# One-query attention over 16 heads on one core: single-head loops with register addresses in place of unrolled pairs

## The chip, the core and the metric

The kernel runs on one NeuronCore of a Trainium2 chip. A core has five engines, each with a queue of its own: TensorE (PE; the profile shows weight loads apart, as PEld), VectorE (DVE), ScalarE (ACT), GpSimd (POOL) and SyncE (SP). In front of each engine a sequencer reads the instructions. It carries out register arithmetic, branches and waits itself and hands the rest to the engine. Rows of the sequencers have a q behind the engine's name (DVEq, ACTq, SPq; PEldq for PE). Data moves between the device memory and the core's SBUF by DMA, sixteen transfer engines that all queues share. [...]

The metric is the device time of one execution, in microseconds; lower is better.

## The reference

One query row per head attends to 8192 keys and values of 256 elements, for 16 heads, in bfloat16:

```python
B, H, Sq, Sk, D = 1, 16, 1, 8192, 256

def reference(q, k, v):
    scale = q.shape[-1] ** -0.5
    scores = jnp.einsum("bhqd,bhkd->bhqk", q, k) * scale
    p = _softmax(scores, axis=-1)
    return jnp.einsum("bhqk,bhkd->bhqd", p, v)
```

K and V are 67 MB each and every element is used once, so the kernel is a stream: 8.39 MB of K and V per head.

## The kernel before

A head's 8192 keys lie as 128 partitions by J = 64 columns of 256 elements; a partition reads 64 consecutive keys. K and V each have two buffers of a whole head (`kbuf0/1`, `vbuf0/1`), taken in turn.

*Transfers.* SP issues all of K and V in a fixed list (`stream`): after a prologue always K of head h+2, then V of head h. A load waits until its buffer is free: K for `kd`, counted when DVE has done the last column of head h-2 of that buffer, V for `pv`, counted by the last P.V matmul (L136). The last heads' V comes in pieces (`V_LATE`), down to two columns at the end.

*Scores.* DVE takes columns 0 to 47 of a head: one instruction per column multiplies the key with the query and sums over the 256 elements (L191, followed by a read of the accumulator), written in place and into `S`. PE takes the other 16, in four groups of four: transpose (L280), copy of the transposes to SBUF by ACT (L376), product with the query as a column (L294), copy of the 16 scores to `S` (L380).

*Softmax.* DVE takes the maximum over `S` (L207), PE transposes it (L228), DVE reduces it to one number (L173), PE spreads it to all partitions (L234), ACT negates it and takes the exponential with a running sum (L384, L388). PE adds the sum over partitions (L244), DVE inverts it (L178).

*Values.* 64 matmuls of one weight column each accumulate P.V (L259) into `acc`; ACT scales the result (L401) and issues a store of 512 B for each head (L408).

*Order.* Every engine has a hardware loop over pairs of heads. A turn is written out for an even and an odd head, so buffers, columns and semaphores of each are constants in the instructions; only wait values, and a few addresses on ACT, are computed in registers. PE's turn is: scores of the even head, P.V of the previous pair's even head, scores of the odd head, P.V of the previous pair's odd head. `_Step` works out the wait values, `AHEAD` counts semaphores up before the loops so that the first turns do not stall. The queue that an instruction stands in is its engine's; nothing is reordered but by the lines below.

## Time and profile before

| | |
|---|---|
| median of 3 runs | 320.04 us (320.0 to 320.32) |
| span of the profiled execution | 318.6 us |
| instructions in it | 6833 |
| PE, PEld, DVE, ACT, POOL busy | 219.2, 156.0, 275.2, 92.5, 1.6 us |
| moved by DMA | 134.29 MB, mean 422 GB/s |
| issue to landing of a whole K, of a whole V | 20.3 us, 28.7 us |
| scores by DVE (L191) | 268.4 us busy |
| P.V (L259) | 147.1 us busy |
| copies of the transposes (L376) | 62.3 us busy |

The profile is one execution; the metric is the median of runs without it, and the execution's own time is the span and what lies around it. In a group's row stand the line, the engine, the operation, the tile that is written and those that are read, the shapes, the count, then busy time and mean duration, then the idle time before the group and what ended it. A row of one line's instructions gives the smallest, median and largest duration in ns and the first and last start in us. A timeline row gives start, duration and count. The waits say who waited for whom: us in total, times, the longest. A window's row gives the stretch, the busy time of PE, PEld, DVE, ACT and POOL with counts, the granted share of TensorE's clock, DMA's share and GB/s. Register and branch instructions have rows but are not counted as busy.

### The profile page before, as it was taken

How to read it: one execution, taken by the hardware profiler on the slowest of the kernel's cores; microseconds unless marked ns; L12 is line 12 of the kernel's file. 1: busy time of each engine (PE TensorE's matmuls, PEld its weight loads, DVE VectorE, ACT ScalarE, POOL GpSimd, SP SyncE). 2: the span in 40 equal slices, each digit the busy share in tenths (PEclk: the TensorE clock that was granted, in tenths of full speed). 3: DMA queues.
4: the chain of work that ended last, by engine and by line, in shares of the span. 5: the costliest groups of instructions: out<-in, count | busy, mean ns of one | idle time of the engine just before them, and what ended most of it. 6: DMA issues, size and time to landing. Idle time of an engine off the chain costs nothing.

```text
span 318.6 us, 6833 instructions
## 1 busy us (share of the span) xinstructions
PE 219.2 (69%) x2163; PEld 156.0 (49%) x2163; DVE 275.2 (86%) x1584; ACT 92.5 (29%) x172; POOL 1.6 (0%) x11
## 2 busy tenths in 40 slices
PE   4446185988775947949387482975739668497987
PEld 1335163656553634727256262663626446266664
DVE  3989999999999898897988979799798897979920
ACT  5436050333215050330505114051330603306010
POOL 1000000000000000000000000000000000000000
PEclk9999999659797875957879597695977859699999
DMA  7999999999999999999999999999999999999995
GB/s 303 447 418 465 393 455 407 448 416 448 412 448 428 428 444 411 453 412 453 420 436 440 416 448 407 453 416 449 424 432 444 411 449 416 444 405 428 419 416 201
DMA packets 6981, 134.29 MB, mean 422 GB/s; under 512 B 800, under 2 KB 1216, under 8 KB 1856
## 3 DMA queue, kind: packets, MB, share of 16 engines
q1 hardware_dynamic: 6912, 134.22, 98.6%
q8 instruction: 2, 0.03, 0.0%
q10 hardware_dynamic: 64, 0.02, 0.0%
q14 instruction: 3, 0.02, 0.0%
HBM read 134.23 MB, written 0.01 MB: 421 GB/s over the span
## 4 chain that ended last, share of the span: by engine, by line
DMA 64%; PE 19%; DVE 15%; SPq 1%; issue 1%; ACT 0%; DVEq 0%; ACTq 0%
DMA vbuf<-in_v_dram 58%; PE acc L259 18%; DVE kbuf L191 14%; DMA kbuf<-in_k_dram 7%; SPq L136 1%; DVE S L191 0%; DVE g L173 0%; PE sm L234 0%; ACT o_sb L401 0%; DVE recip L178 0%; DVEq L209 0%; DVEq L183 0%; PE qps L244 0%; DVE m L207 0%; ACTq L400 0%
## 5 line engine op out<-in xcount | busy, mean ns | idle before, releaser
L191 DVE CUSTOM_DVE_ANT_0 kbuf<-kbuf,q_now 128x256 bf16<-128x256 bf16 x768 | 268.4, 409 | 21.3 <-DMA kbuf<-in_k_dram 20.4
L259 PE MATMUL acc<-vbuf,E 128*1 128x256 bf16 x1024 | 147.1, 313 | 41.6 <-DMA vbuf<-in_v_dram 41.4
L259 PEld LDWEIGHTS acc<-vbuf,E 128*1 128x1 bf16 x1024 | 95.5, 95 | 86.2 <-DMA vbuf<-in_v_dram 44.4
L376 ACT ACTIVATE KT<-tp 128x1024 bf16<-128x1024 bf16 x64 | 62.3, 1021 | 46.4 <-PE tp L280 45.9
L191 DVE DVE_READ_ACCUMULATOR2_ANT S<- 128x1 f32 x768 | 55.2, 72 | 0.0
L280 PE MATMUL tp<-identb,kbuf 128*128 128x128 bf16 x512 | 42.2, 239 | 14.7 <-DMA kbuf<-in_k_dram 14.5
L280 PEld LDWEIGHTS tp<-identb,kbuf 128*128 128x128 bf16 x512 | 33.6, 107 | 18.1 <-DMA kbuf<-in_k_dram 12.1
L294 PE MATMUL spe<-q_now,KT 128*128 128x1 bf16 x512 | 22.9, 166 | 27.3 <-ACT KT L376 27.0
L294 PEld LDWEIGHTS spe<-q_now,KT 128*128 128x128 bf16 x512 | 18.1, 99 | 35.7 <-ACT KT L376 26.1
L401 ACT ACTIVATE o_sb<-acc,recip 1x256 bf16<-1x256 f32 x16 | 7.3, 458 | 87.0 <-PE acc L259 85.7
L384 ACT ACTIVATE negb<-sm 128x1 f32<-128x1 f32 x16 | 2.8, 174 | 83.8 <-PE sm L234 83.8
L173 DVE TENSOR_REDUCE g<-mx 1x1 f32<-1x128 f32 x16 | 4.4, 276 | 7.5 <-PE mx L228 7.5
L234 PE MATMUL sm<-g,ones_row 1*128 1x1 f32 x32 | 6.5, 268 | 5.0 <-DVE g L173 5.0
L228 PE MATMUL mx<-ident,m 128*1 128x128 f32 x32 | 6.5, 287 | 4.3 <-DVE m L207 4.3
L234 PEld LDWEIGHTS sm<-g,ones_row 1*128 1x128 f32 x32 | 5.1, 198 | 7.1 <-DVE g L173 5.6
L371 ACT ACTIVATE q_now<-q_all 128x258 bf16 x16 | 6.7, 418 | 0.1
L178 DVE RECIPROCAL recip<-qps 1x1 f32<-1x1 f32 x16 | 2.4, 152 | 3.9 <-PE qps L244 3.9
L388 ACT ACTIVATE E<-S,negb 128x64 bf16<-128x64 f32 x16 | 5.6, 348 | 0.5
L336 PE MATMUL acc<-q_sb,identb 16*128 16x256 bf16 x16 | 4.3, 404 | 0.8 <-ACT q_all L426 0.8
L228 PEld LDWEIGHTS mx<-ident,m 128*1 128x1 f32 x32 | 2.1, 82 | 5.1 <-DVE m L207 4.8
L426 ACT ACTIVATE q_all<-acc 128x512 bf16<-128x512 f32 x8 | 4.3, 592 | 0.6 <-PE acc L336 0.6
L380 ACT ACTIVATE S<-spe 128x16 f32<-128x16 f32 x16 | 2.9, 184 | 3.6 <-PE spe L294 3.6
(24 smaller groups left out, 18.5 us busy)
## 6 DMA issues: line engine op xcount, KB each, us to landing
kbuf<-in_k_dram SPq DMA_DIRECT2D x15, 4096.0 KB, 20.3
vbuf<-in_v_dram SPq DMA_DIRECT2D x11, 4096.0 KB, 28.7
vbuf<-in_v_dram SPq DMA_DIRECT2D x6, 2048.0 KB, 24.4
vbuf<-in_v_dram SPq DMA_DIRECT2D x5, 1024.0 KB, 14.8
kbuf<-in_k_dram SPq DMA_DIRECT2D x2, 1024.0 KB, 5.8
kbuf<-in_k_dram SPq DMA_DIRECT2D x1, 2048.0 KB, 11.3
vbuf<-in_v_dram SPq DMA_DIRECT2D x1, 768.0 KB, 10.2
vbuf<-in_v_dram SPq DMA_DIRECT2D x1, 640.0 KB, 11.3
```

Of the source, the lines that this page charges most:

```text
L173: dve.tensor_reduce(g[0:1, h.par : h.par + 1], mx[0:1, 0:P], AX.X, ALU.max).then_inc(sem("g"), 1)
L191: ins = dve.tensor_tensor_reduce(out=buf[:, j * D : (j + 1) * D], in0=buf[:, j * D : (j + 1) * D], in1=q_now[h.par][:, 0:D], scale=SCALE, ...
L228: pe.matmul(mx[0:1, 0:P], lhsT=m[:, h.par : h.par + 1], rhs=ident[:, :], start=True, stop=True).then_inc(sem("mT"), 1)
L234: pe.matmul(sm[:, 0:1], lhsT=ones_row[0:1, 0:P], rhs=g[0:1, h.par : h.par + 1], start=True, stop=True,).then_inc(sem("bc"), 1)
L259: ins = pe.matmul(acc[h.par][0:1, 0:D], lhsT=E[h.par][:, j : j + 1], rhs=vbuf[h.par][:, j * D : (j + 1) * D], start=(j == 0), stop=(j == J ...
L280: ins = pe.transpose(tp[gi % 2][:, b * D + hf * P : b * D + (hf + 1) * P], buf[:, j * D + hf * P : j * D + (hf + 1) * P], identb[:, :],)
L294: ins = pe.matmul(spe[:, c : c + 1], lhsT=KT[gi % 2][:, b * D + hf * P : b * D + (hf + 1) * P], rhs=q_now[h.par][:, D + hf : D + hf + 1], ...
L336: ins = pe.matmul(acc[pair % 2][:, (h % 2) * D : (h % 2 + 1) * D], lhsT=identb[0:H, h : h + 1].to_broadcast([H, P]), rhs=q_sb[:, :], start ...
L371: act.activation(out=q_now[h.par][:, :], in_=src_q, func=ACT.Copy).then_inc(sem("qb"), 1)
L376: act.activation(out=KT[gi % 2][:, :], in_=tp[gi % 2][:, :], func=ACT.Copy).then_inc(sem("kt"), 1)
L388: act.activation(out=E[h.par][:, :], in_=S[h.par][:, :], func=ACT.Exp, bias=negb[:, h.par : h.par + 1], scale=1.0, accum_out=lsum[:, h.par ...
L401: act.activation(out=o_sb[h.par][0:1, :], in_=acc[h.par][0:1, 0:D], func=ACT.Copy, scale=recip[0:1, h.par : h.par + 1],).then_inc(sem("fin ...
```

## The change: one head per turn, addresses computed

All four loops now run over single heads. Buffers become one tile of two halves (`kbuf`, `vbuf`, `acc`), `S` and `E` keep all heads, and the place within them is computed in registers from the loop's counter. The parts:

- DVE has an inner loop of six times eight columns; the instruction is `scalar_tensor_tensor` in place of `tensor_tensor_reduce`; the query comes from `q_all` and not from a copy per head. Maximum and reciprocal of earlier heads stand after the second eight. K is freed by the maximum (`m`) and no longer by the last column.
- PE has H + 2 turns: scores of head h, P.V of head h-2 as an inner loop of sixteens, the sum of head h-1. A product with zeros opens each accumulation.
- GpSimd waits for each load in the order of the list and counts it in one of two counters, `kc` (units of eight columns) and `vc` (units of two), for which DVE and PE wait.
- ACT has no query copies per head, and keeps the 16 results in `o_sb`, which one DMA stores at the end.

```diff
-K_FIRST = (16, 32)
-V_LATE = {14: (0, 16, 32, 48), 15: (0, 16, 28, 38, 46, 52, 57, 60, 62)}
+CH = 8
+PC = 16
+V_STEPS = (0, 4, 8, 12, 14)
...
+    15: (0, 16, 28, 40, 46, 52, 56, 60, 62),
+AHEAD = {"vc": 64, "sc": 1, "sp": 2, "m": 1, "pv": 2, "fin": 4, "rc": 3, "l": 2, "qs": 2}
...
-                            sp.wait_ge(sem("kd"), h)
+                        sp.wait_ge(sem("m"), h)
...
+            def landed(kind, name, value, columns):
+                pool.wait_ge(sem(name), value)
+                if kind == "k":
+                    pool.nop().then_inc(sem("kc"), columns // CH)
+                else:
+                    pool.nop().then_inc(sem("vc"), columns // 2)
...
+            with dve.Fori(0, H) as h:
+                par = dve.snap(h % 2)
+                qh = q_all[:, ds(h * D, D)]
+                with dve.Fori(0, NC) as c:
+                    dve.wait_ge(sem("qs"), h // 2 + 3)
+                    dve.wait_ge(sem("kc"), h * KC + c + 1)
+                    for b in range(CH):
+                        col = kbuf[:, ds(par * (J * D) + c * (CH * D) + b * D, D)]
+                        ins = dve.scalar_tensor_tensor(
+                            out=col,
+                            in0=col,
+                            scalar=SCALE,
+                            in1=qh,
                             op0=ALU.mult,
-                            op1=ALU.add,
-                            accum_out=S[h.par][:, j : j + 1],
+                            op1=ALU.mult,
+                            accum_out=S[:, ds(h * J + c * CH + b, 1)],
                         )
                     ins.then_inc(sem("kd"), 1)
+                    with dve.If(c == 1):
+                        with dve.If(h > 0):
+                            xmax(Head(h, 1))
+                        with dve.If(h > 1):
+                            recips(Head(h, 2))
+                dve.wait_ge(sem("kd"), h * NC + NC)
+                dve.wait_ge(sem("sc"), h + 2)
+                dve.tensor_reduce(m[:, :], S[:, ds(h * J, J)], AX.X, ALU.max).then_inc(sem("m"), 1)
...
+            def ktrans(at, gi):
+                for b in range(GRP):
+                    for hf in range(NH):
+                        ins = pe.transpose(
+                            tp[gi % 2][:, b * D + hf * P : b * D + (hf + 1) * P],
+                            kbuf[:, ds(at + (JD + gi * GRP + b) * D + hf * P, P)],
+                            identb[:, :],
+                        )
+                ins.then_inc(sem("tp"), 1)
...
+            with pe.Fori(0, H + 2) as h:
+                with pe.If(h < H):
+                    now = Head(h)
+                    at = pe.snap((h % 2) * (J * D))
+                    with pe.If(h > 0):
+                        transpose_m(Head(h, 1))
+                    pe.wait_ge(sem("kc"), h * KC + KC)
+                    ktrans(at, 0)
+                    ktrans(at, 1)
+                    kscore(now, 0)
+                    with pe.If(h > 0):
+                        bcast(Head(h, 1))
+                    for gi in range(2, NG):
+                        ktrans(at, gi)
+                        kscore(now, gi - 1)
+                    kscore(now, NG - 1)
+                with pe.If(h > 1):
+                    o = pe.snap(Head(h, 2).i)
+                    par = pe.snap(o % 2)
+                    to = acc[0:1, ds(par * 512, D)]
+                    pe.wait_ge(sem("fin"), h + 1)
+                    pe.matmul(to, lhsT=zero[:, 0:1], rhs=zero[:, :], start=True, stop=False)
+
+                    def columns(c, stop):
+                        for b in range(PC):
+                            if b in V_STEPS:
+                                units = (V_STEPS + (PC,))[V_STEPS.index(b) + 1] // 2
+                                pe.wait_ge(sem("vc"), h * VU + c * (PC // 2) + units)
+                            ins = pe.matmul(
+                                to,
+                                lhsT=E[:, ds(o * J + c * PC + b, 1)],
+                                rhs=vbuf[:, ds(par * (J * D) + c * (PC * D) + b * D, D)],
+                                start=False,
+                                stop=stop and b == PC - 1,
+                            )
+                        return ins
+
+                    with pe.Fori(0, J // PC - 1) as c:
+                        columns(c, False)
+                        with pe.If(h == H):
+                            with pe.If(c == 1):
+                                transpose_m(Head(H - 1))
+                            with pe.If(c == 2):
+                                bcast(Head(H - 1))
+                    ins = columns(J // PC - 1, True)
+                    ins.then_inc(sem("pv"), 1)
+                with pe.If(h > 0):
+                    with pe.If(h < H + 1):
+                        total(Head(h, 1))
...
-                    act.dma_start(dst, o_sb[h.par][0:1, :]).then_inc(sem(f"o{h.par}"), 16)
+            act.wait_ge(sem("fin"), H + 4)
+            act.dma_start(out.rearrange("b h s d -> (b s) (h d)"), o_sb[:, :]).then_inc(sem("out"), 16)
+            act.wait_ge(sem("out"), 16)
```

How this stands in the instruction streams is shown at two places. On PE, the start of an odd head's P.V before (L259): two ISA rows, which compute values to wait for, and then matmuls in a row.

```order
L361 COMPARE_AND_BRANCH
L254 ISA
L255 ISA
L259 MATMUL acc<-vbuf,E 1x256 x16
L258 ISA
L259 MATMUL acc<-vbuf,E 1x256 x16
```

The same place of the changed kernel, from the inner loop's start (its lines 331 to 341 are `columns` and the loop around it in the diff).

```order
L341 UNCONDITIONAL_BRANCH
L341 ISA
L332 ISA x2
L332 MATMUL acc<-vbuf,E 1x256
L332 ISA
L332 MATMUL acc<-vbuf,E 1x256
L332 ISA
L332 MATMUL acc<-vbuf,E 1x256
L332 ISA
L332 MATMUL acc<-vbuf,E 1x256
L331 REGISTER_ALU
L332 ISA
```

Every matmul has an ISA row ahead of it. It folds the register operations that give the addresses of its column of `E` and of `vbuf` (add, multiply, add for each); a row of REGISTER_ALU ahead of some gives a value to wait for.

On DVE, within a head before: the branch around an earlier head's reciprocal, and a column (L191), which is the multiply with the sum and the read of the accumulator; the columns behind it follow with nothing between.

```order
L214 COMPARE_AND_BRANCH
L178 RECIPROCAL recip<-qps 1x1
L214 UNCONDITIONAL_BRANCH
L191 ISA kbuf,S<-kbuf,q_now 128x256
L191 ISA S 128x1
```

The start of the inner loop of the changed kernel (its line 214 is the column's instruction, 209 and 211 the loop and the wait).

```order
L209 ISA
L211 ISA
L214 ISA x3
L214 SCALAR_TENSOR_TENSOR kbuf,S<-kbuf,q_all 128x256
L214 ISA
L214 SCALAR_TENSOR_TENSOR kbuf,S<-kbuf,q_all 128x256
L214 ISA
L214 SCALAR_TENSOR_TENSOR kbuf,S<-kbuf,q_all 128x256
```

Here too an ISA row of six register operations stands ahead of each column, five rows stand at the start of each eight, and the loop's counter and two branches at its end.

## The prediction

> **What bounds the kernel now.** I read the page first (span, busy shares, the DMA row), then the chain of waits, then the middle of the run alone, then who waits for whom.

> ```profile
> span 318.6 us, 6833 instructions
> PE 219.2 (69%) x2163; PEld 156.0 (49%) x2163; DVE 275.2 (86%) x1584; ACT 92.5 (29%) x172; POOL 1.6 (0%) x11
> DMA  7999999999999999999999999999999999999995
> q1 hardware_dynamic: 6912, 134.22, 98.6%
> DMA 64%; PE 19%; DVE 15%; SPq 1%; issue 1%; ACT 0%; DVEq 0%; ACTq 0%
> 40.00:280.00 240.00, 169.04 (x1678) 120.48 (x1676) 219.55 (x1265) 68.86 (x126) 0.00 (x0) 0.79 1.00 432
> SPq L136 <- DVE S L191: 240.6, 14, 19.1
> PE acc L259 <- DMA vbuf<-in_v_dram: 41.4, 13, 4.7
> DVE kbuf L191 <- DMA kbuf<-in_k_dram: 20.4, 13, 5.5
> ```

> The transfer engines are full in every slice but the first and last. In the middle they move 432 GB/s; one head is 8.39 MB of K and V, so a head takes 8.39/432 = **19.4 us**, and sixteen of them make the run. SP sits in its waits for buffers only because it issues far ahead of a full queue. PE and DVE both wait for data. So the change is worth nothing until an engine needs more than 19.4 us per head; what each needs today:

> ```profile
> L191 DVE CUSTOM_DVE_ANT_0 kbuf<-kbuf,q_now 128x256 bf16<-128x256 bf16 x768 | 268.4, 409 | 21.3 <-DMA kbuf<-in_k_dram 20.4
> L259 PE MATMUL acc<-vbuf,E 128*1 128x256 bf16 x1024 | 147.1, 313 | 41.6 <-DMA vbuf<-in_v_dram 41.4
> 170.05 1.07 PE L280 MATMUL tp<-identb,kbuf 128*128 128x128 bf16 x16
> 175.03 0.37 PE L294 MATMUL spe<-q_now,KT 128*128 128x1 bf16 x8 [0.55 <-ACT KT L376]
> 165.79 1.91 PE L259 MATMUL acc<-vbuf,E 128*1 128x256 bf16 x16
> ```

> DVE: 268.4 us over 768 columns is 0.35 us each, 48 x 0.35 = 16.8 us per head. PE: scores from 170.05 to 175.40, 5.4 us, and 64 value columns at 147.1/1024 = 0.144 us, 9.2 us; with the small products some 15.5 us. Slack: 2.6 us on DVE, 4 us on PE.

> **The price of an address in a register.** In the kernel before, these engines' addresses are constants. In the changed one nearly every matmul and every DVE column has an ISA row in front (the order rows in the section on the change), which folds two to six register operations into one instruction. The trace has such rows already, at waits and loop starts, with their own durations:

> ```profile
> L255 PEldq FUSED_REGOPS  x16: 37/37/37, 44.7 to 307.7; - x16
> L361 PEldq COMPARE_BRANCH  x1: 68/68/68, 175.0 to 175.0; - x1
> L254 PEldq FUSED_REGOPS  x1: 37/37/37, 175.2 to 175.2; - x1
> L255 PEldq FUSED_REGOPS  x1: 37/37/37, 175.3 to 175.3; - x1
> L288 PEldq ALU_OP  x48: 32/32/42, 15.3 to 290.7; - x48
> L346 PEldq COMPARE_BRANCH  x9: 76/209/223, 30.2 to 316.9; - x9
> L441 ACTq FUSED_REGOPS  x8: 42/43/43, 19.1 to 273.1; - x8
> L433 ACTq FUSED_REGOPS  x8: 50/50/55, 9.2 to 268.5; - x8
> L371 ACTq FUSED_REGOPS  x16: 51/58/65, 19.2 to 292.0; - x16
> 19.07 0.18 ACT L380 ACTIVATE S<-spe 128x16 f32<-128x16 f32 x1 [0.47 <-PE spe L294]
> 19.27 0.42 ACT L371 ACTIVATE q_now<-q_all 128x258 bf16 x1
> L209 DVEq FUSED_REGOPS  x8: 62/63/63, 0.8 to 265.2; - x8
> ```

> Two operations take 37 ns on PE and 43 on ACT, three 50, three or four 51 to 65: about 7 more for each. Six take 37 + 4 x 7 = **65 ns** on PE. L209 on DVE is the same three operations as L433 on ACT, 63 against 50, so DVE pays 1.26 times as much: 1.26 x (43 + 4 x 7) = 90 ns for six. Between such instructions there is a gap: from 19.07 to 19.27 ACT's queue ran L441 (43) and L371 (60) and started an ACTIVATE, so two gaps shared 200 - 103 = 97 ns, some **50 each** (63 on DVE by the same ratio); on PE, L361, L254 and L255 start about 0.1 us apart, which agrees.

> That ACTIVATE itself reads through a register, and it began within the second gap, so one such issue needs no more than the gap. PE issues two per column, a weight load and a matmul. The second is not shown anywhere: at least 0, at most a whole slot of its own like an ALU_OP (32 + 50 = 82 ns) for each of the two. I take one more gap, 50, nearest to the ACT rows.

> **The change part by part.**
> - *PE, value columns.* Per column 65 + 50 + 50 = 165 ns. The branches and waits of each sixteen add: four register additions before waits on the arrival counter, 4 x (36 + 50); two more folded rows at the start, of five and four operations, (58 + 50) + (51 + 50); an untaken `h == H` block that is jumped over, and the jump back, each 209 + 50 (L346 jumps back, 209; L361 falls through, 68); the counter, 86. That is 344 + 209 + 518 + 86 = 1.16 us, 73 ns per column. So 238 ns x 64 = **15.2 us** where 9.2 stood. The sequencer is then slower than the array at either clock (a column takes 1.91/16 = 0.12 us in the row above), so the clock no longer matters here.
> [...]
> - *PE, scores.* 32 transposes with three operations each: 44 + 50 + 27 (half of the second gap: one of the two instructions has a register) = 121 ns against 67. With the copies on ACT in between (1.02 us each, as before) I lay this out to 6.8 us where 5.4 stood.
> - *PE, rest of a turn.* Some eight branches and register rows at 0.09 to 0.26 us, the added product with zeros that opens the accumulation, the three small products: 2.0 us. **Head on PE: 15.2 + 6.8 + 2.0 = 24.0 us**, 4.6 over the transfers.
> - *DVE.* The multiply-and-sum becomes another instruction of the same 256 elements; I keep 0.35 us on the engine (bounds 0.27, an accumulator read fully hidden, to 0.42, nothing hidden: 409 ns is the row's own length). Its sequencer:

> ```profile
> 209.00 0.43 DVE L191 CUSTOM_DVE_ANT_0 kbuf<-kbuf,q_now 128x256 bf16<-128x256 bf16 x1 [0.18 <-DMA kbuf<-in_k_dram]
> L214 DVEq COMPARE_BRANCH  x1: 43/43/43, 209.3 to 209.3; - x1
> L209 DVEq COMPARE_BRANCH  x1: 63/63/63, 148.4 to 148.4; - x1
> L209 DVEq FUSED_REGOPS  x1: 63/63/63, 148.6 to 148.6; - x1
> ```

>   Five instructions (the rest of three columns, each a multiply and a read of the accumulator) were issued between 209.00 and 209.3, 0.06 us each. A column costs 90 + 63 + 2 x 63 = 0.28 us; each eight also start with four more rows (0.5 us), skip a block and jump back (0.2 to 0.3 each, from 148.4 to 148.6) and count: 1.1 us. So 8 x 0.28 + 1.1 = 3.3 us, six times, + 1.8 for the maximum, its wait and the reciprocal: **21.6 us per head**. It is over the transfers too, but under PE, so beside PE it costs nothing.
> - *Waits.* K's buffer is now freed by the maximum, 0.2 us after the last column; K is issued 20.3 us ahead of landing and moves for 9.7, so 10 us cover it. GpSimd's relay adds one or two 0.1 us steps to each arrival and takes landings in the order in which SP issues them; with PE late, data waits for PE. The new wait of DVE on PE's transposed maximum in the second eight is met, if PE is late, by DVE standing there with 4 x 3.3 us still to do in a 24 us turn: covered. ACT loses 16 copies of 0.42 us, off the path.
> - *The end.* One store of 8 KB replaces two of 512 B. From the last copy's start at 316.97 the span has 1.6 us left; the 8 KB load of q took 2.9 us to land, so 0 to +1.8 us, I take +1.

> ```profile
> 2.10 21.10 DMA kbuf<-in_k_dram
> 12.99 0.35 PEld L280 LDWEIGHTS tp<-identb,kbuf 128*128 128x128 bf16 x4 [4.41 <-issue]
> q_sb<-in_q_dram ACTq DMA_DIRECT2D x1, 8.0 KB, 2.9
> 316.97 0.47 ACT o_sb L401
> ```

> **The sum.** PE becomes the bound. Head 0's K is whole at 13.0, head 1's at 23.2 (2.10 + 21.10); scores of head 1 and its turn end at 23.2 + 6.8 + 1.3 = 31.3. Fourteen turns of 24.0: 367.3. The turn with head 14's values, 15.2 + 1.3, and two hooks of head 15 at 0.5: 17.5; head 15's values 15.2 and 0.7 of turn: 15.9; together 400.7. Last copy and store: 1.6 + 1 = 2.6, a span of 403.3. The span of the profiled execution before, 318.6, is 1.4 us under the median of its runs (320.04); with the same around it, **about 405 us**.

> **Rivals.**
> 1. *Every register-addressed PE instruction takes a slot of its own* (82 ns, the upper bound): a value column is 65 + 50 + 164 + 73 = 352 ns, 22.5 us; scores, with 55 ns more on each of 32 transposes and some of it under ACT's copies, 8.2; head 32.7. 31.3 + 1.4 + 14 x 32.7 + 24.8 + 23.2 + 2.6 + 1.4 = 543; with half of that excess 474. For it: FUSED_REGOPS and ALU_OP rows are never closer than a gap on any queue. Against it: ACT's ACTIVATE. [...]
> 2. *DVE is the bound, PE cheaper*: with the second PE issue at 0, a PE head is 64 x 0.188 + 6 + 2 = 20.0, under DVE's 21.6. Then 16 x 21.6 + 5.5 (first column at 5.5) = 351, and behind head 15's maximum half of head 14's values, the exponential and all of head 15's: 6 + 2 + 12 + 3 = 23. About 376; DVE's bounds (20 to 23) make it 350 to 395.
> 3. *Not slower: the register work is hidden.* If the sequencers fold addresses while the engines work through queued instructions, and a column costs PE under (19.4 - 5.4 - 2.0)/64 = 0.19 us all told and DVE under (19.4 - 1.8)/48 = 0.37, the transfers still bound: 318 to 322, by the store, the start and the end. For it: both engines have a queue. Against it: 0.24 and 0.41 by the rows above; a queue hides a burst, not a mean.

> **Chances.** The forecast (385 to 440) 0.45; rival 1 (440 to 545) 0.23; rival 2 (345 to 385) 0.21; rival 3 0.08, of which half within 0.2%, which is about what these measurements can tell from no change; something else 0.03. Faster 0.04, same 0.04, slower 0.92. The range leaves out rival 3 and the upper third of rival 1: 345 to 500.

> **What would show it.** Right: the DMA row well under 9 from the first tenth on; PE's P.V matmuls evenly 0.16 to 0.19 us apart with a pause of about 0.6 us after each sixteen; FUSED_REGOPS near 65 ns on PE and 90 on DVE; DVE waiting for PE in its second eight; PE no longer waiting for V. If DVE's columns are 0.35 apart and DMA still reads 9, rival 3; if PE waits for DVE's maximum, rival 2; columns 0.3 apart, rival 1. It would be wrong if folded operations cost less when they follow each other than the lone ones I could read, or if register operands are resolved beside the previous instruction.

## The result and the profile after

The changed kernel takes 410.88 us (median of four runs, 410.8 to 411.24) where the kernel before takes 320.1: 1.284 times as long, 95% interval 1.282 to 1.286. The profiled execution has a span of 409.5 us. In the order in which the lines of before were read, the page of the changed kernel, and of the middle of its run the same window view:

```profile
span 409.5 us, 10729 instructions
PE 313.9 (77%) x2178; PEld 169.5 (41%) x2178; DVE 279.4 (68%) x1584; ACT 88.8 (22%) x154; POOL 1.6 (0%) x11
DMA  8999989979796979969696997979697891733600
q1 hardware_dynamic: 6912, 134.22, 78.9%
PE 69%; issue 16%; ACT 6%; DVE 5%; DVEq 3%; DMA 1%; ACTq 0%
```

```profile
60.00:380.00 320.00, 262.16 (x1815) 141.01 (x1814) 228.40 (x1295) 67.55 (x118) 0.00 (x0) 0.81 0.81 335
```

The chain has turned over: DMA held 64% of it, now PE holds 69%, and 16% is "issue", time in which an engine waits for nothing that the profile shows. The transfers move 335 GB/s where they moved 432, and PE's granted clock in the middle is no lower than before (0.81 against 0.79). PE has 15 more matmuls in this trace and 95 us more of busy time, as matmuls that follow each other more slowly overlap less: P.V's 1024 last 308 ns each (313 before) and cover 200.6 us where they covered 147.1. Who waits for whom, in the changed kernel:

```profile
DVE g L200 <- PE mx L240: 55.1, 14, 9.6
PE acc L332 <- issue: 37.4, 64, 1.3
DVE kbuf L214 <- issue: 29.9, 29, 1.1
PE mx L240 <- DVE m L231: 11.0, 2, 6.9
PE sm L244 <- DVE g L200: 7.4, 2, 3.7
```

PE waits for no V any more. P.V (L332) waits 64 times for issue, once for each sixteen of columns. DVE waits 14 times for PE's transposed maximum: 9.6 us once, behind the last head, and (55.1 - 9.6)/13 = 3.5 us a head before. PE waits for DVE only four times, all of them in the first turns. One turn of PE, and the rows of the two loops' sequencers within a turn (smallest, median and largest duration in ns):

```profile
186.28 0.19 PE L251 MATMUL qps<-ones_col,lsum 128*1 128x1 f32 x2
187.42 2.15 PE L258 MATMUL tp<-identb,kbuf 128*128 128x128 bf16 x16
193.99 0.38 PE L272 MATMUL spe<-q_col,KT 128*128 x8 [0.69 <-ACT KT L359]
195.10 3.57 PE L332 MATMUL acc<-vbuf,E 128*1 x16 [0.34 <-issue]
...
199.05 3.02 PE L332 MATMUL acc<-vbuf,E 128*1 x16 [0.38 <-issue]
203.02 3.02 PE L332 MATMUL acc<-vbuf,E 128*1 x16 [0.96 <-issue]
206.62 3.04 PE L332 MATMUL acc<-vbuf,E 128*1 x16 [0.58 <-issue]
209.75 0.19 PE L251 MATMUL qps<-ones_col,lsum 128*1 128x1 f32 x2
```

```profile
L332 PEldq FUSED_REGOPS  x73: 42/74/143, 194.9 to 219.0; - x73
201.24 0.23 PEld L332 LDWEIGHTS acc<-vbuf,E 128*1 x2 [0.17 <-issue]
L343 PEldq COMPARE_BRANCH  x3: 207/207/212, 197.9 to 205.8; - x3
L341 PEldq COMPARE_BRANCH  x3: 76/207/209, 198.2 to 206.2; - x3
L214 DVEq FUSED_REGOPS  x64: 59/93/222, 194.9 to 219.0; - x64
L214 DVE SCALAR_TENSOR_TENSOR kbuf<-kbuf,q_all x51: 417/422/427, 194.7 to 218.8; - x51
```

The four sixteens of P.V take 3.95, 3.97, 3.60 and 3.1 us from start to start; the third has no jump back behind it, the last stands outside the loop. Two weight loads of 79 ns side by side span 0.23 us, so a column takes 0.23 - 0.08 = 0.15 us (152 ns in most of the trace's pairs) where nothing but columns is issued and the granted clock is full: 16 x 0.152 = 2.4, and the other 1.5 us of a looped sixteen are its register rows, waits and jumps. From 190.1 to 200.3 us the granted clock is 0.5, and the later columns of the first sixteen stand 213 ns apart (it is busy for 3.57 us); yet it takes no longer than the second, most of which runs at 1.0. Scores run from 187.42 to 194.37, 7.0 us. PE's turns are even, and the row of one line shows their length (two matmuls each, so 28 are 14 turns):

```profile
L251 PE MATMUL qps<-ones_col,lsum x28: 163/163/164, 69.1 to 373.8; 128*1 128x1 f32 x28
```

(373.8 - 69.1)/13 = 23.44 us per head.

### The profile page after: what moved, and what is told of

Read it like the earlier page. It is cut to its first block, busy times and chain, and to the rows that moved or that the text cites. A ratio compares the mean times of both kernels' runs of the same rounds, so it can differ in the third digit from the quotient of the medians.

```text
span 409.5 us, 10729 instructions
## 1 busy us (share of the span) xinstructions
PE 313.9 (77%) x2178; PEld 169.5 (41%) x2178; DVE 279.4 (68%) x1584; ACT 88.8 (22%) x154; POOL 1.6 (0%) x11
## 3 DMA queue, kind: packets, MB, share of 16 engines
q1 hardware_dynamic: 6912, 134.22, 78.9%
## 4 chain that ended last, share of the span: by engine, by line
PE 69%; issue 16%; ACT 6%; DVE 5%; DVEq 3%; DMA 1%; ACTq 0%
PE acc L332 49%; PE tp L258 11%; ACT KT L359 6%; DVE kbuf L214 5%; PE spe L272 3%; PE sm L244 2%; DVEq L214 2%; PE acc L325 1%; PE mx L240 1%; DMA q_sb<-in_q_dram 1%; PE qps L251 1%; DVEq L209 0%; DVEq L211 0%; ACT o_sb L381 0%; ACT q_all L399 0%
## 5 line engine op out<-in xcount | busy, mean ns | idle before, releaser
L214 DVE SCALAR_TENSOR_TENSOR kbuf<-kbuf,q_all x768 | 268.9, 421 | 36.5 <-issue 29.9
L332 PE MATMUL acc<-vbuf,E 128*1 x1024 | 200.6, 308 | 37.5 <-issue 37.4
L332 PEld LDWEIGHTS acc<-vbuf,E 128*1 x1024 | 87.4, 85 | 152.1 <-issue 91.3
L258 PE MATMUL tp<-identb,kbuf 128*128 128x128 bf16 x512 | 67.5, 275 | 2.0 <-POOLq L174 1.9
L214 DVE DVE_READ_ACCUMULATOR kbuf<-kbuf,q_all x768 | 63.0, 82 | 0.0
L258 PEld LDWEIGHTS tp<-identb,kbuf 128*128 x512 | 49.5, 116 | 14.2 <-issue 6.0
L200 DVE TENSOR_REDUCE g<-mx 1x128 f32 (+1 forms) x16 | 4.4, 278 | 55.1 <-PE mx L240 55.1
L272 PE MATMUL spe<-q_col,KT 128*128 x512 | 25.7, 169 | 16.6 <-ACT KT L359 16.0
L272 PEld LDWEIGHTS spe<-q_col,KT 128*128 128x128 bf16 x512 | 21.4, 107 | 24.7 <-ACT KT L359 17.1
L240 PE MATMUL mx<-ident,m 128*1 128x128 f32 x32 | 6.7, 295 | 19.2 <-DVE m L231 11.0
L381 ACT ACTIVATE o_sb<-acc,recip (+1 forms) x16 | 7.4, 465 | 36.7 <-PE acc L332 32.9
L244 PE MATMUL sm<-g,ones_row 1*128 (+1 forms) x32 | 8.4, 330 | 7.7 <-DVE g L200 7.4
## 6 DMA issues: line engine op xcount, KB each, us to landing
vbuf<-in_v_dram SPq DMA_DIRECT2D x6, 2048.0 KB, 19.4
```

The source lines that it names most:

```text
L214: ins = dve.scalar_tensor_tensor(out=col, in0=col, scalar=SCALE, in1=qh, op0=ALU.mult, op1=ALU.mult, accum_out=S[:, ds(h * J + c * CH + b, ...
L240: pe.matmul(mx[0:1, 0:P], lhsT=m[:, :], rhs=ident[:, :], start=True, stop=True).then_inc(sem("mT"), 1)
L244: pe.matmul(sm[:, 0:1], lhsT=ones_row[0:1, 0:P], rhs=g[0:1, ds(h.i, 1)], start=True, stop=True).then_inc(sem("bc"), 1)
L258: ins = pe.transpose(tp[gi % 2][:, b * D + hf * P : b * D + (hf + 1) * P], kbuf[:, ds(at + (JD + gi * GRP + b) * D + hf * P, P)], identb[: ...
L272: ins = pe.matmul(spe[:, c : c + 1], lhsT=KT[gi % 2][:, b * D + hf * P : b * D + (hf + 1) * P], rhs=q_col[:, ds(h.i * NH + hf, 1)], start= ...
L332: ins = pe.matmul(to, lhsT=E[:, ds(o * J + c * PC + b, 1)], rhs=vbuf[:, ds(par * (J * D) + c * (PC * D) + b * D, D)], start=False, stop=st ...
```

## The experiments

The theory after this reading: PE's sequencer sets the 23.4 us, by addresses, waits and jumps alike, and everything else is hidden beneath it. Its rivals: DVE's register work, or one of the other parts of the change (GpSimd's relay, K freed by the maximum, the single store, the place of DVE's hooks, which are the maximum and the reciprocal of earlier heads that it takes between a head's columns).

**PE without registers.** PE's turns written out, nothing else changed:

```diff
-            with pe.Fori(0, H + 2) as h:
-                with pe.If(h < H):
+            for h in range(H + 2):
+                if h < H:
...
-                    at = pe.snap((h % 2) * (J * D))
+                    at = (h % 2) * (J * D)
...
-                    with pe.Fori(0, J // PC - 1) as c:
+                    for c in range(J // PC - 1):
```

> PE's eighteen turns are written out one after the other with constant addresses and waits; DVE, ACT, GpSimd and SP stay as in the changed kernel. Theory (PE's register work sets the 23.47 us turn, 14.65 to 15.1 of it P.V): a PE head falls to some 15.5 us as before the change, PE waits for data again, and the larger of DVE (about 19.5 us of own work per head in the changed kernel's trace) and the transfers (19.4) sets the pace: about 325 us (318 to 335). Rival A (DVE's register work is nearly as slow as forecast, 21.6 us per head): 345 to 376. Rival B (GpSimd's relay, K freed by the maximum, or the handshake between PE and DVE sets the turn): 390 or more.

Measured 328.89 us, 1.027 times the kernel before (1.0242 to 1.0297): 82 of the 90.8 us are gone with PE's turns written out alone. Both rivals' numbers are missed. DVE's maxima, one a head, show what sets the pace now, early and late in the run:

```profile
L231 DVE TENSOR_REDUCE m<-S x7: 219/220/221, 79.8 to 192.1; 128x1 f32 x7
L231 DVE TENSOR_REDUCE m<-S x5: 219/219/220, 230.6 to 308.5; 128x1 f32 x5
```

(192.1 - 79.8)/6 = 18.7 us a head, DVE's own pace with registers (19.5 was expected), until it has caught up with the data; then (308.5 - 230.6)/4 = 19.5, the pace of the transfers.

**DVE without registers.** The same for DVE's heads and eights:

```diff
-            with dve.Fori(0, H) as h:
-                par = dve.snap(h % 2)
+            for h in range(H):
+                par = h % 2
...
-                with dve.Fori(0, NC) as c:
+                for c in range(NC):
...
```

> DVE's heads and eights are written out with constants; PE and the rest stay as in the changed kernel. Theory (DVE is under PE and costs nothing beside it): 407 to 412 us, with DVE waiting longer for PE's transposed maximum (5 us or more per head, 3.9 now). Rival A (DVE bounds, or each head pays DVE's register work through the handshake): 380 to 400.

407.82 us, as expected. PE's turn has not moved, (370.5 - 66.0)/13 = 23.42 us; the whole run only starts earlier (the first of these rows stood at 69.1):

```profile
L251 PE MATMUL qps<-ones_col,lsum x28: 163/163/164, 66.0 to 370.5; 128*1 128x1 f32 x28
```

**P.V alone without registers.** The single-head loop stays; P.V stands twice, for each half of the buffers, behind a branch:

```diff
+                    for p in range(2):
+                        with pe.If(par == p):
+                            to = acc[0:1, p * 512 : p * 512 + D]
...
+                            for j in range(J):
...
+                                    lhsT=E[:, p * J + j : p * J + j + 1],
+                                    rhs=vbuf[:, p * J * D + j * D : p * J * D + (j + 1) * D],
```

> The loop stays one of single heads; only P.V is written out for the two halves of the buffers behind a branch each, with constant addresses (E has two halves too); scores keep their registers. Theory: a PE head is 7.0 (scores) + 9.2 to 9.6 (64 columns at the array's pace, the additions before the waits hidden by queued matmuls) + 0.4 (branches) + 1.3 = 18 us, under the transfers: 320 to 335 us, 326 taken. Rival (the additions and waits, not the columns' addresses, hold PE: 20 rows of 0.09 us per head are not hidden): PE head 19.8, 335 to 345. Rival A (DVE's register work): 345 to 376.

327.53 us (1.0218 to 1.0288 times before), where the theory put it. The 64 value columns are the change's price: this edit gives back as much as writing out all of PE does. The additions before the waits are still there, but 64 columns now take 9.0 to 9.9 us (two heads between 110 and 139 us), so the rival by which the additions hold PE (19.8 us a head) is missed too. PE's turn is now (287.0 - 81.6)/11 = 18.7 us, and so is DVE's (below): the loop of DVE, registers and all, keeps just ahead of the transfers' 19.4.

```profile
L251 PE MATMUL qps<-ones_col,lsum x24: 163/166/167, 81.6 to 287.0; 128*1 128x1 f32 x24
L231 DVE TENSOR_REDUCE m<-S x12: 219/220/221, 79.8 to 285.8; 128x1 f32 x12
```

**The price of a wait, of the inner loop, of an address in the scores.** Three edits of the changed kernel. One wait a sixteen:

```diff
-V_STEPS = (0, 4, 8, 12, 14)
+V_STEPS = (0,)
```

> The changed kernel with one wait per sixteen value columns where five stood: four register additions and four waits less per sixteen. Theory (PE's sequencer sets the time, and each addition has a slot of its own, 36 + 50 ns): 16 x 0.086 = 1.4 us less per head, 22 over the run: 385 to 392 us. Rival (the additions are hidden behind queued matmuls): 408 to 412.

The four sixteens written out, registers kept:

```diff
-                    with pe.Fori(0, J // PC - 1) as c:
+                    for c in range(J // PC - 1):
                         columns(c, False)
-                        with pe.If(h == H):
-                            with pe.If(c == 1):
+                        if c == 1:
+                            with pe.If(h == H):
...
```

> The changed kernel without the inner loop: a head's four sixteens are written out, with addresses still in registers from the head's counter, and the block for the last turn stands behind a branch in two of the four. Gone per head: three jumps back and counters, one of three jumped blocks, and the longer rows at the start of each sixteen. Theory (a looped sixteen takes 3.95 us, the written-out last one 3.1 to 3.2 in the trace): three times 0.75 less, two jumped blocks of 0.27 stay as against three: 2.0 us less per head and 32 over the run: 372 to 386 us, 379 taken. Rival (jumps are prefetched or overlapped with the array): 400 to 411.

The scores written out for two halves:

```diff
+                    for p in range(2):
+                        with pe.If(half == p):
+                            at = p * (J * D)
+                            ktrans(at, 0)
...
```

> The changed kernel with PE's scores written out for the two halves of K's buffer behind a branch each: the 32 transposes have constant addresses, the 32 products keep their register for the query. Theory (the sequencer sets the scores' 7.0 us): transposes fall from 0.124 to 0.067 us, scores to 5.2 to 6.0 with ACT's copies in between, + 0.35 for branches: 1.0 to 1.5 us less per head: 386 to 396 us. Rival (ACT's copies set the scores): 408 to 413.

Measured 384.48, 368.46 and 402.52 us: all three outside the ranges of their theories (385 to 392, 372 to 386, 386 to 396), the first two below, the third above, and none where its rival puts it. The same row as above in each of the three, in this order:

```profile
L251 PE MATMUL qps<-ones_col,lsum x28: 163/163/163, 67.5 to 350.2; 128*1 128x1 f32 x28
```

```profile
L251 PE MATMUL qps<-ones_col,lsum x28: 163/163/164, 66.5 to 337.3; 128*1 128x1 f32 x28
```

```profile
L251 PE MATMUL qps<-ones_col,lsum x28: 163/163/164, 69.2 to 365.3; 128*1 128x1 f32 x28
```

Turns of 21.75, 20.83 and 22.78 us, against 23.44. So sixteen additions with their waits are worth 1.69 us a turn, 0.106 us each (0.086 expected). Three passes of the inner loop and one jumped block are worth 2.6 (2.0 expected). The transposes' addresses are worth only 0.66: the scores shrink to between 5.6 and 6.1 us, but the two branches take some 0.4 back, and ACT's copies are waited for again:

```profile
PE spe L272 <- ACT KT L362: 19.1, 28, 0.9
```

(9.7 us in the changed kernel, both between 90 and 330 us.) The first two rivals, by which this work is hidden, are out: each row that goes shortens the turn. Of these two the sizes came out a quarter to a third larger than expected. That of the scores (1.0 to 1.5 expected) came out at about half, and its rival, that ACT's copies set the scores, is half right: they take over as soon as the sequencer lets go.

**Where DVE's hooks stand.** In the changed kernel alone, and in the one with P.V in halves:

```diff
-                    with dve.If(c == 1):
+                    with dve.If(c == 0):
                         with dve.If(h > 0):
                             xmax(Head(h, 1))
```

> The changed kernel with the same one edit: maximum and reciprocal after the first eight. Theory (PE's sequencer sets the 23.47 us turn, and DVE only waits there for PE): 404 to 410 us; what is gained is at the start, where PE waits 3.7 us twice for DVE. Rival (the handshake between DVE and PE is part of every turn): 390 or less.

> The kernel with P.V written out in two halves (327.5 us), and DVE's maximum and reciprocal of the earlier heads after the first eight columns where they stood after the second. Theory (with PE fast, a new wait sets the end: PE's spread of the maximum stands ahead of P.V in its queue and waits 2.4 us per head for DVE, so V's buffers come free late and the transfers run dry for some 5 us, around head 2 and ahead of the last V): the wait goes, 321 to 324 us. Rival (DVE's loop with registers sets what is left): 327 to 328 as before this edit.

408.39 us for the changed kernel: 2.5 us, all at the start (its row of L251 runs from 66.3 to 371.0, the same 23.44 us a turn). 325.46 us for P.V in halves, 2.1 less than without the edit, 1.5 more than the theory's range and 1.5 less than the rival's. PE's wait for DVE's maximum falls from 36.2 to 14.4 us, so the wait was real; but it was worth only some 2 us, since DVE stands in the chain with the edit (39% of it DVE, 24% issue, 19% DVE's sequencer) as it did without it (38%, 23%, 18%). The first of these is of P.V in halves, the second with the early hooks as well:

```profile
PE sm L244 <- DVE g L200: 36.2, 15, 3.7
```

```profile
PE sm L244 <- DVE g L200: 14.4, 14, 1.1
DVE 39%; issue 24%; DVEq 19%; PE 9%; DMA 7%; ACT 1%; ACTq 0%; POOLq 0%
```

**Both engines without registers.** The two first edits together:

> Both PE and DVE written out with constants; what is left of the change is the relay by GpSimd, K freed by the maximum, the other DVE instruction, ACT's loop, E and S for all heads, and the single store. Theory (these cost nothing): 318 to 323 us, transfers full. Rival (one of them costs): 327 or more, with gaps in the transfers' row.

334.32 us, 1.044 times before (1.0418 to 1.0457): a clear miss, and 5.4 us slower than with DVE's registers left in. The last places to look were the hooks (PE waits 51.2/15 = 3.4 us there for DVE in each head) and the program's length, so I removed the first and tested the second apart. The hooks' wait in this kernel:

```profile
PE sm L244 <- DVE g L200: 51.2, 15, 3.8
```

> P.V in two halves, DVE's heads written out with constants, and the maximum and reciprocal after the third column as in the kernel before. Theory (DVE's registers cost nothing here, as its columns stay 0.346 us apart; DVE's code adds 13 packets of 8 KB at 0.33 us to one engine, 4 us at most): 320 to 324 us, at most 2 us from the kernel with the loop and the early maximum. Rival (DVE's register work still costs about 1 us per head): 315 to 319, or the looped one stays 4 us or more above it.

In the kernel before, with PE's nine turns of a pair written out:

```diff
-                with pe.Fori(0, H // 2 + 1) as i:
+                for i in range(H // 2 + 1):
...
```

> The kernel before with PE's nine turns written out one after the other, constant waits, nothing else. PE has less to do and waits for data as before. Theory (a long written-out program is fetched through a transfer engine: 17 packets of 16 KB of about 1.06 us each where a loop has 2; one of the sixteen engines falls behind by about 1 us per 20 us, and each load waits for it): 9 us at most by the end, 324 to 330 us, and the sixteenth arrival of a late load 6 to 9 us after the fifteenth. Rival (the fetches cost nothing; the kernel with both engines written out was slow for the place of the maximum alone): 319.8 to 321.

332.36 us and 322.96 us, and neither is what its theory or its rival said. With the early hooks PE no longer waits for them (51.2 us in the kernel above; what is left of its waits for DVE are two for the maximum over `S`, 10.0 us), and the kernel is still slow, so the hooks are not it. Its row of DVE's maxima, early and late, then its queues and GB/s:

```profile
L231 DVE TENSOR_REDUCE m<-S x3: 220/220/220, 78.1 to 112.3; 128x1 f32<-128x64 f32 x3
```

```profile
L231 DVE TENSOR_REDUCE m<-S x9: 220/220/221, 132.1 to 294.3; 128x1 f32<-128x64 f32 x9
```

```profile
GB/s 317 447 412 451 408 407 411 368 425 425 422 445 438 425 425 422 441 441 430 433 413 442 441 433 426 417 441 438 433 429 414 445 441 426 407 404 413 114 391 128
q14 instruction: 13, 0.11, 0.1%
q8 instruction: 2, 0.03, 0.0%
```

While data lie ready DVE needs (112.3 - 78.1)/2 = 17.1 us a head. Once it waits for data it gets a head every (294.3 - 132.1)/8 = 20.3 us, where the transfers' pace is 19.4, and near the end one slice moves only 114 GB/s. Each load adds sixteen counts to its semaphore, as many as the profile counts transfer engines, and the trace has their times: in this kernel the sixteenth count comes 0.6 us after the fifteenth at 115 us, 4.4 at 206, 8.3 at 310. In the kernel with both engines written out it comes 9.1 us late at 307 us; in the one with P.V in halves and DVE's loop kept, within 0.2 us from the third head on. One of the sixteen shares, and so by this reading one transfer engine, falls behind by 0.8 to 0.9 us a head, and every load waits for it. What the two slow kernels share is DVE's written-out program, with 13 fetches of 8 KB on the queue called q14 (of the kind "instruction" in the row above). PE's long program, 17 fetches of 16 KB on q8, costs less: in the kernel before with PE written out the sixteen counts of a load lie within 3.4 us of each other (2.0 in the kernel before) until the last four pieces of V (4.8), and the time grows by 2.8 us (1.0066 to 1.01 times).

The times of the counts tie the lag to the fetches. In the kernel with P.V in halves and DVE written out, the last count of a load stands 3.0 us behind the first at 115 us and 10.8 us behind at 302 us, and it gets there in eight steps of 0.9 to 1.0 us. There are eight fetches on q14 in this stretch, each step is in the first load to land behind one of them, and in the eleven loads with no fetch ahead of them nothing moves. The other fifteen counts stay where they are: all these fetches delay the same share. A fetch of PE in the kernel before written out delays one count too, by about 1.4 us, but not the same one as the fetch ahead of it: at 300 us eight of the sixteen are 2.9 to 3.4 us behind the first and none is further. By these counts the larger fetches cost less because their delays are spread over the shares. Where the transfers have time to spare it does not matter: with DVE alone written out the same 13 fetches leave no lag that grows (the sixteenth count is at most 2.5 us behind the fifteenth, 0.1 at the end). Why a fetch that lasts 0.3 us costs its share a whole microsecond is not shown.

**The single store** in the kernel before, nothing else:

```diff
-                    act.wait_ge(sem("fin"), h.of(1, 5))
-                    act.dma_start(dst, o_sb[h.par][0:1, :]).then_inc(sem(f"o{h.par}"), 16)
...
+                act.wait_ge(sem("fin"), H + 4)
+                act.dma_start(out.rearrange("b h s d -> (b s) (h d)"), o_sb[:, :]).then_inc(sem("o0"), 16)
```

> The kernel before with the single store alone: the sixteen results stay in one row and one DMA of 8 KB stores them at the end. Theory (the changed kernel's trace has 1.9 us from the last copy's start to the end of the span, the kernel before 1.6): +0.3 us, 319.8 to 320.8 us. Rival, as the prediction took it: +1 us, 321; up to +1.8.

320.57 us, 1.0011 times before (1.0001 to 1.002), so 0.3 us.

No kernel of these beats the one before; the nearest of the single-head loops, P.V in halves with the early hooks, stays 1.6% behind.

## Where the prediction was right and where not

**The bound and the sign: right.** PE became the bound and nothing else did: with PE's turns written out 82 of 90.8 us are given back, with DVE's heads 3. The time, 410.88 for 405, lies in the likeliest case and its own span of 385 to 440. That it came within 6 us is in part luck: an error of 13.8 us at the start and one of 7.3 us in the turns have opposite signs (below).

**PE's head: 23.44 us for 24.0.** P.V takes 23.44 - 8.8 = 14.6 (15.2 predicted), scores 7.0 (6.8), the rest 1.8 (2.0).
- Column: 152 ns for 165, by the trace of the changed kernel. The folded row of six operations (L332) takes 74 ns where 65 were worked out from rows of two to four; which of the operations costs more is not shown. But the second issue of a column costs 152 - 74 - 50 = 28 and not another whole gap (in the trace the weight load starts 50 ns behind the folded row, the matmul 7 ns behind the weight load, the next folded row 21 ns behind the matmul). So the doubtful term lay near its lower bound, and rival 1 (a slot for each) is out. With its share of waits and jumps a column takes 14.6/64 us, 229 ns, where 238 were predicted.
- Extras of a sixteen: 1.5 us for 1.16. An addition with its wait costs 0.106 for 0.086, and the folded rows at a sixteen's start are up to 143 ns long where 51 and 58 were taken. Taken jumps last 207 to 212 ns, as read from L346, and the one that falls through 76 (L343 and L341 in the rows above). These errors cancel in part: the prediction has 15.2/4 = 3.8 us for every sixteen; the first two take 0.15 more, the third 0.2 and the last 0.7 less, as the loop runs three times and not four, with no jump back behind the third.
- Clock: "so the clock no longer matters here" came out nearly right (sixteens of 3.95 us at 0.5 and 3.97 at 1.0, turns of 23.3 to 23.6 us), but the row behind it, 0.12 us a column, has the clock at 1.0 alone. At 0.5 columns of the kernel before stand 213 ns apart, where they stand 109 apart at 1.0. That is more than the 152 ns of a column's issue; only with the waits and jumps, 229 ns, is the sequencer the slower one at both.

**DVE: 18.7 us a head, not 21.6.** Covered by PE as predicted, so it didn't hurt the sum, but the step that sized it failed: "a column costs 90 + 63 + 2 x 63 = 0.28 us". The folded row is 93 ns, but folded rows of successive columns stand 0.197 us apart where nothing holds them: the gap and both issues take 0.104 us where 0.189 were taken. So the sequencer has its extra rows of most eights done while the engine, at 0.35 us a column, is still busy (it waits for issue only at the first and the third eight of a head, 1.0 and 1.1 us), and the head stays near the 17.1 us that it takes with constants. Registers and branches cost DVE 1.6 us a head and not 4.8. Hence rival 2 ("about 376", 350 to 395) fails even with PE written out, where the run takes 328.89: DVE is faster than the transfers. The other instruction costs nothing (421 ns on the row for 409, columns still 0.35 apart).

**The waits: right in the middle, wrong at the start.** "DVE standing there with 4 x 3.3 us still to do in a 24 us turn: covered": DVE does stand there, 3.5 us a head. But the step took PE to be late from the first turn. In turns 1 and 2 (the first is turn 0) PE is early and waits for DVE's second eight and for its maximum:

```profile
31.02 0.57 PE L244 MATMUL sm<-g,ones_row 1*128 x2 [3.71 <-DVE g L200]
42.60 0.59 PE L240 MATMUL mx<-ident,m 128*1 128x128 f32 x2 [6.93 <-DVE m L231]
49.61 0.58 PE L244 MATMUL sm<-g,ones_row 1*128 x2 [3.70 <-DVE g L200]
```

That is 14.3 us. The sum had turn 2 end at 31.3 + 24.0 = 55.3; it ends at 69.1. This is the mis-sized term of the sum: +13.8 at the start, 13 x (23.44 - 24.0) = -7.3 in the turns, and -0.3 for the last two turns and the end. Together they make the 6 us by which 405 was short. By the prediction's own signs "PE waits for DVE's maximum" meant rival 2; it happened in two turns without DVE being the bound, so that sign was too coarse.

**The store:** 0.3 us for +1, within 0 to 1.8. **The relay and K freed by the maximum:** no experiment takes them out alone. With P.V in halves and early hooks all of them are in place, and the run is 5.3 us over the kernel before (320.17 in the same series), DVE's pace included; unless another part of the change gains time there, they cost no more. The relay's own price can be read: where DVE waits for K, its first column starts 0.14 us behind the last count with both engines written out, and 0.02 or 0.16 us, from head to head in turn, in the kernel before.

**Rival 3** (hidden by queues) is out on PE, by the price experiments, and nearly right on DVE, where a column of engine work (0.346 us) is 1.8 times as long as its issue (0.197).

## What to carry to other kernels

Count what the sequencer does per engine instruction before folding unrolled code into a loop with computed addresses: here six folded operations, a weight load and a matmul came to 152 ns, over the 109 ns that a column takes the array at the full granted clock, and waits and jumps added half as much again. An engine with a column every 0.35 us hid the same addresses, one with a column every 0.14 us on average did not, so put constants back in the innermost line of the short one only (P.V in two halves gave back nine tenths of the loss). And do not write everything out: with the transfers full, each fetch of DVE's longer program put one share of the transfers 1 us further behind, and the kernels with it were 5 to 7 us slower.
